# Unused tiles shift where three stages' matmul operands start in SBUF

## The chip, the cores and the metric

The kernel runs on one core of a Trainium2 chip. The metric is the device time of one execution in microseconds (us). The kernel before took 562.35 us, the median of three runs (561.91 to 562.72).

## The reference, cut to what matters

Three layers follow each other, in float32:

```python
# 1. attention, 2 x 8 heads, 768 positions, 64 dims: only keys in the query's hash bucket count
mask   = q_bucket[:, :, :, None] == k_bucket[:, :, None, :]     # 6 bits, sign of q @ proj, k @ proj
scores = np.where(mask, scale * q @ k.T, -1e9)
attn   = exp(scores - max(scores)); x = (attn / (sum(attn) + 1e-9)) @ v
# 2. a dense layer on 1536 tokens of 512
h    = x @ w_in                         # to 1024
solu = h * softmax(h)
ln   = (solu - mean(solu)) / sqrt(var(solu) + 1e-6) * g_ln
x    = ln @ w_out                       # back to 512
# 3. one of 8 experts for each token
e   = argmax(x @ w_gate)
out = gate * sigmoid(x @ w_output_gate)[e] * (relu(x @ w1[e]) @ w2[e])
```

## The kernel before, in words

The order of the work is written out by hand (`tc.manual_schedule()`): each engine runs its instructions in the order in which the functions issue them, and semaphores join the engines.

**Numbers in two parts.** Most products are made of float32r operands: a value x is kept as a high part (tiles whose names begin with H, or end in h) and a low part (L, or l), and a product is the sum of high x high, high x low and low x high. A TensorE matmul here has a stationary operand, which an LDWEIGHTS brings into the array (128 columns of 4 bytes from each partition), and a moving operand that is streamed past it (256, 384 or 512 columns of 4 bytes). In the profile's rows PE is the streaming, PEld the loading of the next stationary operand, which runs beside it. In the names of L243 the moving operand stands first: `ps<-Hk,Hq` streams Hk past Hq.

**Attention** (`Attention`, up to about 208 us). Eight pairs of heads, one in partitions 0 to 63 and one in 64 to 127, so that matmuls come in pairs that run side by side in the two halves of the array (`both`, L239). For each pair of heads `rowmax` (L247) makes masked scores with k moving and q stationary (every third column of q) for VectorE to take row maxima of; `score` (L269) makes them again with q moving and k stationary, four products each (Hk Hq, Hk Lq, Lk Hq, and Fk Fq for the mask and the maximum). ScalarE takes the exponential, GpSimd adds up denominators, `av` (L288) multiplies by v in plain float32. The tiles of q and k come from the pool `op`: `turn` (L174) makes Hk and Hq, `low` (L183) Lk and Lq, `mask` (L222) Fk and Fq, two buffers each.

**The dense layer** (`Ffn`, about 211 to 372 us). Twelve tiles of 128 tokens. `up` (L636) streams the parts of W_in (`wi`) past the parts of x (`xh`, `xl`, pool `xp`); `turn` (L689) transposes the gated activations into `lh` and `ll` (pool `lp`); `down` (L702) streams the parts of W_out (`wo`) past `lh` and `ll`. Both go through `gemm` (L628), whose matmuls stand at L634. The last token tile goes through `down2` with 256 columns at a time.

**The experts** (`Experts`, from about 373 us). Each expert's weights come by DMA, are cut into `wh` and `wl`, and are used twice: `up` (L1216, matmuls at L1231) streams the tokens' `xh` and `xl` (pool `xe`; for expert 0 the two buffers of tile `e` in pool `ep`), 256 columns, past `wh` and `wl`; `down` (L1243, matmuls at L1253) streams `wh` and `wl`, 512 columns, past the hidden values, which lie in W_out's old tiles `wo`.

**Places.** A pool lays its tiles one behind the other in each partition's memory, each at a multiple of 32 bytes, and the pools stand one on the other; so the size of a tile sets where all later ones start. Nothing in the kernel before asks for a certain start.

Of the kernel before, what the change touches and what calls it, by code (L numbers as in the profile page):

```python
# [8 lines left out]
F32 = mybir.dt.float32  # L9
# [7 lines left out]
P = 128  # L17
# [102 lines left out]
class Attention:  # L120
    def __init__(self, tc, ctx, q, k, v, xT):
        self.tc, self.nc = tc, tc.nc
        self.src = dict(q=q, k=k, v=v)
        self.xT = xT
        pool = lambda n, b, **kw: ctx.enter_context(tc.tile_pool(name=n, bufs=b, **kw))
        self.nat = pool("nat", 1)
        self.op = pool("op", 2)
        self.ap = pool("ap", 1)
        self.sp = pool("sp", 2)
        self.st = {}  # L130
        self.pt = []
        pp = pool("pt", 1)
        for i in range(NPT):
            self.pt.append(pp.tile([P, 2, HW + 2], F32, name=f"pt{i}"))
        self.npt = self.nmax = 0
        self.maxima = [pp.tile([P, 3, 2, 3], F32, name=f"m{i}") for i in range(2)]

    def preset(self):
# [5 lines left out]
    def open(self, ctx):  # L144
        self.order = self.pools = [
            ctx.enter_context(self.tc.tile_pool(name=f"ps{n}", bufs=1, space=PSUM)) for n in range(4)
        ]
        self.order = self.pools[1:]
        self.aside = self.pools[0]
        self.filler = self.new(self.aside)[:, 0]  # L150
# [23 lines left out]
    def turn(self, j):  # L174
        nc, st = self.nc, self.st[j]
        for nm in "kq":
            hi = self.op.tile([P, 2, HW], F32R, tag="H" + nm, name="H" + nm)
            nc.scalar.copy(hi, st["T" + nm])
            st["H" + nm] = hi.rearrange("p i n -> p (i n)")
            if j == 0:  # L180
                self.low(0, nm, nc.gpsimd)

    def low(self, j, nm, eng):  # L183
        st = self.st[j]
        t = self.op.tile([P, 2, HW], F32R, tag="L" + nm, name="L" + nm)
        st["L" + nm] = t.rearrange("p i n -> p (i n)")
        eng.tensor_tensor(
            out=st["L" + nm], in0=st["T" + nm].rearrange("p i n -> p (i n)"), in1=st["H" + nm].bitcast(F32), op=ALU.subtract
        )
# [32 lines left out]
    def mask(self, j):  # L222
        nc, st = self.nc, self.st[j]
        ps = [self.wide() for _ in range(2)][::-1]
        for i in range(2):
            for x, o in ((1, D), (0, 0)):
                r = slice(o, o + D)
                nc.tensor.matmul(
                    ps[x][:, i], self.C["tab"][r, i + 2 * x, :], st["bits"][r], start=True, stop=True, tile_position=(o, 0)
                )  # L230
        for x, nm in ((1, "k"), (0, "q")):
            t = self.op.tile([P, 2, HW], F32R, tag="F" + nm, name="F" + nm)
            if x:
                nc.scalar.activation(out=t, in_=ps[x], func=AF.Relu)
            else:
                nc.vector.tensor_copy(t, ps[x])
            st["F" + nm] = t.rearrange("p i n -> p (i n)")

    def both(self, ps, jobs):  # L239
        for n, (w, x) in enumerate(jobs):  # L240
            for h in range(2):
                r = slice(D * h, D * h + D)
                self.nc.tensor.matmul(  # L243
                    ps[:, h], w[r], x[r], start=(n == 0), stop=(n == len(jobs) - 1), tile_position=(D * h, 0)
                )
# [321 lines left out]
def apart(tc, group, ins, gap):  # L567
    ins = ins.ins
    tc.nc.gpsimd.memset(gap, 0.0)
    tc.declare_no_dep(ins, group=group, reason="the rows that these DMAs write are disjoint")  # L570
    tc.add_to_no_dep_group(group, ins)
# [18 lines left out]
class Ffn:  # L590
# [3 lines left out]
    def __init__(self, tc, ctx, C, xT, W, scratch, cnt, ep, ex):  # L594
        self.tc, self.nc, self.C, self.xT, self.ex = tc, tc.nc, C, xT, ex
        self.scratch, self.base, self.W = scratch, cnt, W
        nc = self.nc
        pool = lambda n, b, **kw: ctx.enter_context(tc.tile_pool(name=n, bufs=b, reuse_waits="tile", **kw))
        self.xp = pool("xp", 2)
        self.ep = ep  # L600
        self.lp = pool("lp", 2)
        self.gp = pool("gt", 1)
        self.sp = pool("sp2", 3)
        self.ph = pool("ph", 2, space=PSUM)
        self.pt = pool("ptr", 2, space=PSUM)
        self.py = pool("py", 1, space=PSUM)
        self.pl = pool("pl", 1, space=PSUM)
        self.lg = self.pl.tile([P, 512], F32, name="lg")
        self.st, self.grp, self.sent, self.turned = {}, {}, [], []
        self.wi = W.wi  # L610
        self.wo = W.wo
        self.iota = self.gp.tile([P, CAP], F32, name="iota")
        self.spot, self.st_row, self.split_row, self.low = {}, {}, {}, []
# [475 lines left out]
class Experts:  # L1089
# [23 lines left out]
    def open(self, ctx):  # L1113
        pool = lambda n, b, **kw: ctx.enter_context(self.tc.tile_pool(name=n, bufs=b, reuse_waits="tile", **kw))
        self.rp = pool("rp", 3)
        self.xp = pool("xe", 2)
        self.sp = pool("se", 4)
        self.px = pool("pxe", 2, space=PSUM)
        self.pg = pool("pg", 2, space=PSUM)
        self.po = pool("po", 1, space=PSUM)  # L1120
# [244 lines left out]
@with_exitstack  # L1365
def tile_kernel(
    ctx: ExitStack, tc, q, k, v, proj, moe_w_in, moe_w_out, moe_g_ln, moe2_w_gate, moe2_w_output_gate, moe2_w1, moe2_w2, out
):
    nc = tc.nc
    cp = ctx.enter_context(tc.tile_pool(name="cp", bufs=1))  # L1370
    scratch = tc.dram_tile([SLOTS + N, ROW], F32, name="scratch")
    cnt = cp.tile([P, E], F32, name="cnt")

    def clear(z, n):
        nc.sync.dma_start(
            out=scratch[4 * P * n:4 * P * (n + 1), :].rearrange("(p a) r -> p (a r)", p=P).rearrange("p (b x) -> p b x", b=10),
            in_=z.unsqueeze(1).to_broadcast([P, 10, 2 * ROW // 5]),
        )

    def blank(z):  # L1380
        nc.gpsimd.memset(z, 0.0)
        for n in range(3):
            nc.sync.dma_start(
                out=out[4 * P * n:4 * P * (n + 1), :].rearrange("(p a) r -> p a r", p=P),
                in_=z.unsqueeze(1).to_broadcast([P, 4, DM]),
            )

    with tc.manual_schedule(), ExitStack() as c0, ExitStack() as c4:
        c1 = c0.enter_context(ExitStack())
        xp = c1.enter_context(tc.tile_pool(name="xT", bufs=1, side="right"))  # L1390
        xT = xp.tile([P, 2, 4, S], F32, name="xT")
        keep = c4.enter_context(tc.tile_pool(name="wo", bufs=1))
        W = Weights(tc, cp, xp, keep, moe_w_in, moe_w_out, moe_g_ln, moe2_w_gate, moe2_w_output_gate)
        with ExitStack() as c2:
            cv = c2.enter_context(tc.tile_pool(name="cv", bufs=1))
            at = Attention(tc, c2, q, k, v, xT)
            at.load(0, "qk")
            at.C = C = {}
            at.open(c2)
            make_consts(tc, cp, cv, proj, C)  # L1400
            at.preset()
            nc.gpsimd.tensor_copy(cnt, C["first"])
            nc.gpsimd.memset(W.wg, 0.0)
            at.warm(10)
            at.tables()
            at.warm(1)
            z = cv.tile([P, 2 * ROW // 5], F32, name="zero")
            nc.gpsimd.memset(z, 0.0)
            extra = W.steps(cv, at.bank)
            at.run(8, extra, [lambda n=n: clear(z, n) for n in range(7)])  # L1410
        stg = c4.enter_context(tc.tile_pool(name="ws", bufs=4, reuse_waits="tile"))
        ep = c4.enter_context(tc.tile_pool(name="ep", bufs=2, reuse_waits="tile"))
        r0 = c4.enter_context(tc.tile_pool(name="r0", bufs=1, reuse_waits="tile"))
        ex = Experts(tc, C, stg, moe2_w1, moe2_w2, scratch, out, r0, W.wo)
        with ExitStack() as c2:
            ffn = Ffn(tc, c2, C, xT, W, scratch, cnt, ep, ex)
            for u in range(4):
                ex.fetch(u)

            def ahead():  # L1420
                c1.close()
                return ex.ahead(c0)

            ffn.run(ahead, blank)
        with ExitStack() as c2:
            ex.open(c2)
            ex.run(lambda: counts(tc, C, cnt))
    overflow(tc, C, moe2_w1, moe2_w2, scratch, out, ex.done)
# [36 lines left out]
```

## Time and profile before

| | us |
|---|---|
| median of three runs | 562.35 |
| profiled execution | 562.85 |
| its span, first to last instruction | 561.0 |
| PE busy in the span | 548.5 (98%) |
| DVE, POOL, ACT busy | 394.9, 330.7, 268.4 |

The profiled execution was 0.5 us over the median; 1.85 us of it lie outside its span. A row of a source line gives each kind of instruction with its count and the shortest, median and longest duration of one. A matmul's duration includes a tail that lies under the next matmul, so the time from one start to the next is shorter than the duration. The timeline joins neighbours of the same kind: its second column runs from the first one's start to the last one's end.

### The profile page before, as it was taken

Reading aid. Unit: us, or ns where it says so; the run is one execution under the profiler, and the core shown is the slowest. Engines: PE = TensorE matmul, PEld = TensorE weight load, DVE = VectorE, ACT = ScalarE, POOL = GpSimd, SP = SyncE. Lnnn points to the kernel's source line nnn. Section 1 sums busy time; section 2 is a strip of 40 time slices with the busy share of each in tenths; the row PEclk is TensorE's granted clock in tenths of the full one; section 3 lists DMA queues with packets and bytes.
Section 4 is the critical chain, followed back from the end, with each engine's and each line's share of the span. In section 5 each row is a group of like instructions: output and inputs, shape, how many; then the busy total and the mean of one; then the engine's idle time right before and its main releaser. Section 6 shows DMA issues by size and latency. Waiting matters only on the chain. (4 is left out here: it accounts for less than half of the span.)

```text
span 561.0 us, 9939 instructions
## 1 busy us (share of the span) xinstructions
PE 548.5 (98%) x3850; PEld 437.8 (78%) x3850; DVE 394.9 (70%) x793; ACT 268.4 (48%) x456; POOL 330.7 (59%) x270
## 2 busy tenths in 40 slices
PE   8899999999999999999999999999999999999995
PEld 3776667776667747788888888899989989899894
DVE  7978888888988756766687777776674664656631
ACT  3457657575665651233223323637455463463530
POOL 5389898898989883000000050327785965958741
PEclk9899999999999999999999999999999999999999
DMA  3555636465452535600000040139829467497201
GB/s 112 155 148 146 161 128 194 135 160 145 158 143 81 129 108 221 224 1 1 1 1 0 1 96 0 76 101 365 301 74 339 141 243 258 152 332 253 78 23 36
DMA packets 48100, 76.09 MB, mean 136 GB/s; under 512 B 11563, under 2 KB 20523, under 8 KB 48046
## 3 DMA queue, kind: packets, MB, share of 16 engines
q1 hardware_dynamic: 42910, 59.50, 33.3%
q10 hardware_dynamic: 2896, 9.57, 5.6%
q0 software_dynamic: 2240, 6.31, 3.5%
q8 instruction: 32, 0.52, 0.4%
q14 instruction: 22, 0.18, 0.1%
HBM read 58.39 MB, written 17.93 MB: 136 GB/s over the span
## 5 line engine op out<-in xcount | busy, mean ns | idle before, releaser
L1143 POOL TENSOR_TENSOR wl<-ws,wh 128x512 fp32r<-128x512 f32 x75 | 107.5, 1467 | 40.1 <-ACT wh L1141 39.4
L283 POOL TENSOR_TENSOR acc<-pt,pt 128x768 f32<-128x768 f32 x48 | 89.9, 1873 | 29.3 <-ACT pt L279 29.3
L255 DVE TENSOR_REDUCE m<-ps 128x2 f32<-128x768 f32 x96 | 87.9, 949 | 12.0 <-PE ps L243 9.5
L279 ACT ACTIVATE pt<-ps 128x768 f32<-128x768 f32 x96 | 76.4, 813 | 38.1 <-PE ps L243 38.0
L1253 PE MATMUL o<-wh,wo 128*128 128x512 f32 x256 | 82.5, 394 | 0.0
L1141 ACT CAST wh<-ws 128x512 fp32r<-128x512 f32 x120 | 66.2, 619 | 6.0 <-POOL wl L1143 4.7
L294 PE MATMUL ps<-pt,v 128*64 128x385 f32 x384 | 67.1, 493 | 0.0
L616 POOL TENSOR_TENSOR xl<-xT,xh 128x512 fp32r<-128x512 f32 x12 | 15.4, 1288 | 86.4 <-ACT xh L625 56.3
L1143 DVE TENSOR_TENSOR wl<-ws,wh 128x512 fp32r<-128x512 f32 x45 | 53.8, 1222 | 10.5 <-ACT wh L1141 10.3
L1237 DVE SCALAR_TENSOR_TENSOR wo<-g,wo 128x512 fp32r<-128x512 f32 x32 | 22.1, 691 | 51.9 <-ACT wo L1236 51.9
L285 POOL TENSOR_TENSOR acc<-acc 128x768 f32<-128x768 f32 x30 | 54.8, 1827 | 2.4
L1253 PEld LDWEIGHTS o<-wh,wo 128*128 128x128 f32 x256 | 48.1, 188 | 9.7
L1236 ACT ACTIVATE wo<-g 128x512 fp32r<-128x512 f32 x32 | 19.1, 598 | 75.1 <-PE g L1231 69.4
L294 PEld LDWEIGHTS ps<-pt,v 128*64 128x64 f32 x384 | 25.6, 136 | 34.3 <-issue 30.4
L1253 PE MATMUL o<-wl,wo 128*128 128x512 f32 x128 | 50.1, 391 | 0.0
L634 PE MATMUL h<-wi,xh 128*128 128x512 f32 x192 | 49.4, 399 | 0.0
L634 PE MATMUL y<-wo,lh 128*128 128x512 f32 (+1 forms) x176 | 41.5, 387 | 0.0
L634 PEld LDWEIGHTS h<-wi,xh 128*128 128x128 f32 x192 | 34.9, 188 | 7.4 <-ACT xh L625 0.6
L797 POOL DMA_INDIRECT scratch<-row,slot x12 | 12.0, 999 | 48.3 <-DVE slot L824 23.2
L243 PE MATMUL ps<-Hk,Hq 64*128 64x384 f32 x192 | 37.0, 374 | 1.1 <-DVE m L255 0.5
L634 PEld LDWEIGHTS y<-wo,lh 128*128 128x128 f32 x176 | 31.5, 188 | 7.2 <-issue 0.2
L243 PE MATMUL ps<-Hq,Hk 64*128 64x384 f32 x192 | 35.4, 364 | 1.0 <-DVE m L255 1.0
(240 smaller groups left out, 1157.4 us busy)
## 6 DMA issues: line engine op xcount, KB each, us to landing
ws<-in_moe_w_dram SPq DMA_DIRECT2D x32, 1024.0 KB
scratch<-zero SPq DMA_DIRECT2D x7, 1030.0 KB
r<-scratch SPq DMA_DIRECT2D x16, 257.5 KB
raw<-in_moe_w_in_dram ACTq DMA_DIRECT2D x8, 512.0 KB
raw<-in_moe_w_out_dram ACTq DMA_DIRECT2D x8, 512.0 KB
v<-in_v_dram SPq DMA_DIRECT2D x8, 384.0 KB
out_dram<-zero SPq DMA_DIRECT2D x3, 1024.0 KB
q<-in_q_dram SPq DMA_DIRECT2D x7, 384.0 KB
```

What stands on the lines that cost most here:

```text
L243: self.nc.tensor.matmul(ps[:, h], w[r], x[r], start=(n == 0), stop=(n == len(jobs) - 1), tile_position=(D * h, 0))
L255: nc.vector.tensor_reduce(out=st["m", i][:, c, :, kh], in_=ps, axis=AX.X, op=ALU.max, negate=True)
L279: nc.scalar.activation(out=pt[:, :, 0:HW], in_=ps, func=AF.Exp, scale=0.125)
L283: nc.gpsimd.tensor_tensor(out=acc, in0=st["pt", i, c - 1][:, :, 0:HW], in1=pt[:, :, 0:HW], op=ALU.add)
L285: nc.gpsimd.tensor_tensor(out=acc, in0=parts.pop(), in1=acc, op=ALU.add)
L294: nc.tensor.matmul(st["x", i][D * h:D * h + D, 0:HW + 1], st["v"][:, h, c, :], st["pt", i, c][:, h, 0:HW + 1], start=(c == 0), stop=(c == ...
L634: nc.tensor.matmul(ps, a[:, k, :], w[j](k), start=(n == 0), stop=(n == len(jobs) - 1))
L1141: nc.scalar.copy(hi[:, k, :], t[:, k, :])
L1143: eng.tensor_tensor(out=lo[:, k, :], in0=t[:, k, :], in1=hi[:, k, :].bitcast(F32), op=ALU.subtract)
L1236: nc.scalar.activation(out=hi, in_=ps, func=AF.Relu)
L1237: nc.vector.scalar_tensor_tensor(out=hl[:, 2 * g:2 * g + 2, :], in0=ps, scalar=0.0, in1=hi.bitcast(F32), op0=ALU.max, op1=ALU.subtract)
L1253: nc.tensor.matmul(st["o"][t], h[:, f, t * P:(t + 1) * P], w[:, f % 4, :], start=(f == 0 and n == 0), stop=(f == 7 and n == 2),)
```

## The change

Ten tiles that nothing writes or reads are put into pools, and so later tiles start elsewhere:

```diff
+        self.gaps = []                                             # Attention.__init__
...
@@ Attention.turn, behind the low part of the first k and of the first q, and Attention.mask, behind Fk and Fq
             if j == 0:
                 self.low(0, nm, nc.gpsimd)
+                self.apart(16 if nm == "k" else 48)
+
+    def apart(self, n):
+        self.op.tile([P, n], F32, tag=f"apart{n}{len(self.gaps)}", name="apart", bufs=1)
+        self.gaps.append(n)
...
             st["F" + nm] = t.rearrange("p i n -> p (i n)")
+            if j == 0:
+                self.apart(16 if nm == "k" else 48)
...
@@ Ffn.__init__
         self.lp = pool("lp", 2)
         self.gp = pool("gt", 1)
+        self.lp.tile([P, 56], F32, name="shift", bufs=1)
+        self.gp.tile([P, 8], F32, name="rest")
...
@@ Experts.open
         self.xp = pool("xe", 2)
+        self.xp.tile([P, 8], F32, name="shift", bufs=1)
...
@@ tile_kernel
         r0 = c4.enter_context(tc.tile_pool(name="r0", bufs=1, reuse_waits="tile"))
+        ep.tile([P, 8], F32, name="shift", bufs=1)
+        r0.tile([P, 56], F32, name="rest")
```

The starts of the matmuls' operands in a partition, modulo 256 bytes, as the built programs have them:

| stage | moving | stationary | before: moving, stationary | after |
|---|---|---|---|---|
| scores, `score` | Hq, Lq, Fq | Hk, Lk, Fk | 128, 128 | 192, 128 |
| scores, `rowmax` | Hk, Fk | Hq, Fq | 128, 128 | 128, 192 |
| W_in product | wi | xh, xl | 224, 224 | 224, 224 |
| W_out product | wo | lh, ll | 160, 224 | 160, 192 |
| experts' `up` | xh, xl, e | wh, wl | 160, 224 | 192, 224 |
| experts' `down` | wh, wl | hidden, in wo | 224, 160 | 224, 160 |

The slices that one matmul reads begin whole multiples of 256 bytes further on (in `rowmax` the stationary ones 0, 4 or 8 bytes beyond that). Tiles behind the new ones that are not in the table move by 256 or 512 bytes, or by 32 bytes more or less; some, like `lt` and `id`, are small.

The instructions of PE, DVE, ACT and POOL are the same, in the same order and with the same waits. On SP the order of the DMAs is the same too; what differs is which of them waits. In what is executed the one place is in the experts' `rows`, which loads the routed tokens of experts 1 and 2 (`r`, four DMAs) into memory that earlier tiles leave. Before:

```order
L1185 DMA r_4515<-scratch 128x515 [waits DMAHW3_49,DVE_49,PE_49]
L1185 DMA r_4518<-scratch 128x515 [waits DMAHW4_49,DVE_49,PE_49]
L1185 DMA r_4521<-scratch 128x515 [waits DMAHW5_49]
L1185 DMA r_4524<-scratch 128x515 [waits DMAHW6_49]
L1130 DMA ws<-in_moe_w_dram 128x4x512 [waits DVE_49] x2
```

And with the change:

```order
L1196 DMA r_4524<-scratch 128x515 [waits DMAHW3_49,DVE_49,PE_49]
L1196 DMA r_4527<-scratch 128x515 [waits DMAHW4_49,PE_49]
L1196 DMA r_4530<-scratch 128x515 [waits DMAHW5_49]
L1196 DMA r_4533<-scratch 128x515 [waits DMAHW6_49,DVE_49,PE_49]
L1141 DMA ws<-in_moe_w_dram 128x4x512 [waits DVE_49] x2
```

The wait for DVE that stood ahead of the second DMA now stands ahead of the fourth, with one for PE.

## Rows read from the trace of the kernel before

**Rows 1.** Busy time of the engines in attention, dense layer, experts.
```profile
core 0: us, PE busy (x) PEld busy (x) DVE busy (x) ACT busy (x) POOL busy (x), PEclk, DMA share, GB/s
13.00:208.00 195.00, 192.04 (x1659) 132.39 (x1659) 160.96 (x219) 120.50 (x177) 166.46 (x92) 0.99 0.51 143
224.00:366.00 142.00, 141.32 (x805) 116.89 (x804) 104.17 (x341) 48.58 (x95) 20.98 (x28) 1.00 0.13 41
374.00:545.00 171.00, 171.00 (x1160) 156.46 (x1161) 102.47 (x139) 86.14 (x160) 123.43 (x105) 1.00 0.61 212
```

**Rows 2.** What PE waited for, longest in total first.
```profile
PE ps L243 <- DVE m L255: 1.5, 3, 1.0
PE ps L228 <- DVE bits L220: 1.4, 2, 0.9
PE ps L195 <- DVE fill L46: 1.3, 1, 1.3
```

**Rows 3.** Timeline of PE, W_in product: start, length, what, count.
```profile
213.87 1.98 PE L634 MATMUL h<-wi,xh 128*128 128x512 f32 x8
...
222.03 1.30 PE L634 MATMUL h<-wi,xh 128*128 128x512 f32 x5
```

**Rows 4.** Timeline of PE, W_out product.
```profile
241.70 3.89 PE L634 MATMUL y<-wo,lh 128*128 128x512 f32 x16
```

**Rows 5.** Timeline of PE, experts' up.
```profile
397.95 0.62 PE L1231 MATMUL g<-xh,wh 128*128 128x256 f32 x4
...
403.85 0.62 PE L1231 MATMUL g<-xh,wl 128*128 128x256 f32 x4
```

**Rows 6.** Timeline of PE, experts' down.
```profile
407.93 0.62 PE L1253 MATMUL o<-wh,wo 128*128 128x512 f32 x2
...
411.36 0.62 PE L1253 MATMUL o<-wh,wo 128*128 128x512 f32 x2
```

**Rows 7.** Timeline of PE, attention's scores.
```profile
149.84 0.34 PE L243 MATMUL ps<-Hk,Hq 64*128 64x384 f32 x2
...
150.55 0.34 PE L243 MATMUL ps<-Hq,Hk 64*128 64x384 f32 x2
...
151.24 0.34 PE L243 MATMUL ps<-Hk,Hq 64*128 64x384 f32 x2
151.42 0.34 PE L243 MATMUL ps<-Fk,Fq 64*128 64x384 f32 x2
```

**Rows 8.** Matmuls by line and form: busy us, mean ns.
```profile
L195 PE MATMUL ps<-fill 64*128 64x512 bf16 x2 | 0.6, 376 | 0.0
```

**Rows 9.** Timeline of PE, two bfloat16 filler matmuls.
```profile
7.91 0.59 PE L195 MATMUL ps<-fill 64*128 64x512 bf16 x2
```

**Rows 10.** Line 634, the dense layer's products: shortest, median, longest ns.
```profile
L634 PE MATMUL h<-wi,xh x192: 387/393/501, 211.0 to 342.8; 128*128 128x512 f32 x192
L634 PE MATMUL y<-wo,lh x176: 276/394/496, 229.3 to 362.2; 128*128 128x512 f32 x160, 128*128 128x256 f32 x16
L634 PE MATMUL y<-wo,ll x88: 281/394/400, 233.0 to 364.0; 128*128 128x512 f32 x80, 128*128 128x256 f32 x8
L634 PE MATMUL h<-wo,lh x32: 276/379/484, 351.7 to 366.3; 128*128 128x512 f32 x16, 128*128 128x256 f32 x16
L634 PE MATMUL h<-wo,ll x16: 276/338/398, 356.3 to 367.2; 128*128 128x512 f32 x8, 128*128 128x256 f32 x8
```

**Rows 11.** Line 1231, experts' up, the same columns.
```profile
L1231 PEld LDWEIGHTS g<-xh,wh x224: 187/188/188, 396.3 to 543.0; 128*128 128x128 f32 x112
L1231 PE MATMUL g<-xh,wh x224: 276/276/280, 396.6 to 543.1; 128*128 128x256 f32 x112
L1231 PE MATMUL g<-e,wh x64: 276/276/388, 373.3 to 384.6; 128*128 128x256 f32 x64
```

**Rows 12.** Line 243, attention's scores; below, what PE and PEld waited for there.
```profile
L243 PE MATMUL ps<-Hq,Lk x192: 330/331/518, 18.5 to 206.1; 64*128 64x384 f32 x192
...
  DVE m L255: 7.4, 15
```

**Rows 13.** Timeline of SP, the experts' first rows.
```profile
377.35 1.78 SPq L1185 DMA_DIRECT2D r<-scratch  x4
```

**Rows 14.** Line 1200, the transposes that read such rows.
```profile
L1200 PE MATMUL x<-ident,r x56: 271/272/273, 391.6 to 529.0; 128*128 128x128 f32 x56
```

## The prediction

> **What bounds the kernel now.** I read the engines' busy time by stage first. In attention PE is busy 192.0 of 195 us, in the dense layer 141.3 of 142, among the experts 171 of 171, at a granted clock of 0.99 to 1.00, its upper level; no other engine is over 85% in any of them [rows 1]. The list of waits agrees: the longest that PE itself waited for one cause is 1.5 us in total [rows 2]. So the end is set by how fast matmuls follow each other, and the next view is the timeline of PE, from which I take the time from one start to the next, and divide it by the columns streamed, to compare stages:
>
> - W_in product: 36 matmuls of 512 columns start between 213.87 and 222.03, so 226.7 ns each, 0.443 ns a column [rows 3].
> - W_out product: 16 take 3.89 us with the last one's 0.394 [rows 4, 10], so (3.89 - 0.394) / 15 = 233.1 ns, 0.455 a column.
> - Experts' up: 52 of 256 columns between 397.95 and 403.85, 113.5 ns, 0.443 a column [rows 5].
> - Experts' down: 15 between 407.93 and 411.36, 228.7 ns, 0.447 a column [rows 6].
> - Attention's scores: 9 pairs of 384 columns between 149.84 and 151.42, 175.6 ns a pair, 0.457 a column; the four pairs of `rowmax` before 150.55 take 177.5 each [rows 7].
> - bfloat16 filler, half as many bytes a column: 0.59 - 0.376 = 0.214 us for 512, 0.418 a column [rows 8, 9].
>
> Products of the same kind of operands thus run at 0.443 to 0.457 ns a column, 3% apart, and the filler 6% below the best. Nothing in the waits explains that: streaming itself is slower in places, while the next stationary operand is read from the same memory beside it. Where the operands start is one thing that differs between these stages. The two stages with the highest figure, attention and W_out, are both touched by the change, and so is experts' up, which has the lowest.
>
> **The change part by part.** It adds and removes no instruction. What it can do is alter these spacings, and a change of one is felt in full, since PE has no slack to absorb it.
>
> Attention: 6 kinds of 192 matmuls, 576 pairs. If q's new place brings them to the lowest level that such operands have, 0.4427 x 384 = 170.0 ns, a pair gains 5.6 ns: 576 x 5.6 = 3.2 us. The shortest typical duration among them, 331 ns for Hq past Lk [rows 12], shows that some already run near that. Bounds: at the filler's 0.418, 160.5 ns, the gain is 15.1 x 576 = 8.7 us; upward, W_out's product, whose operands lie 64 apart as these now will, runs 0.0125 ns a column over W_in's, whose lie at 0, and that on 384 columns is 4.8 ns, a loss of 2.8 us. I take 3.2, the level that two other stages hold steadily. Not all is kept: the weight loads of these lines already wait 7.4 us in 15 places for VectorE's maxima [rows 12], and a faster `rowmax` arrives earlier. I give back half of what its 192 pairs gain, 0.5 us. GpSimd and VectorE, at 166 and 161 of 195 us [rows 1], can follow a stage that is 1.4% shorter.
>
> W_out: 160 + 80 + 16 + 8 = 264 matmuls of 512 columns [rows 10]. From 233.1 to 226.7 ns is 6.4 x 264 = 1.7 us. Bounds: at the filler's 214 ns 5.0 us gained; one more such step upward, 1.7 lost. The 48 of 256 columns are at 276 to 281 ns at their shortest [rows 10], the same as experts' up, and count nothing.
>
> Experts' up: 8 experts x 8 blocks x 12 = 768 matmuls, at 276 ns median with hardly any spread [rows 11]. They are at the lowest level already, so I take 0. Bounds: at the filler's rate 107 ns, 6.5 x 768 = 5.0 us gained; at the 281 ns that is the shortest of `y<-wo,ll` [rows 10], which has the same width, 5 x 768 = 3.8 us lost.
>
> W_in's product and experts' down keep their distance: 0. VectorE, ScalarE and GpSimd also read and write the shifted tiles; no row has such an operand at another start, but they are idle 15% of a stage or more [rows 1], which covers a few per cent. The moved SP waits cost nothing: the four loads are issued within 1.78 us from 377.35, and what reads them first starts at 391.6 [rows 13, 14]; were DVE's wait late there, the weights queued behind on SP would be late too, but SP passed that same wait as its second of four.
>
> Sum: 3.2 - 0.5 + 1.7 = 4.4 us off the profiled execution's 562.85, and since that stood 0.5 us over the median, 562.35 - 4.4 = 558.0 as the median of runs.
>
> **One rule against it.** The Trainium skill, page "SBUF — State Buffer", section "Who interferes with whom", gives TensorE two read ports, one for the moving operand and one for LDWEIGHTS, that are independent, and says that PE never waits on anyone. No run here shows ports; by that rule there would be no conflict between the operands and the gain would be 0. The skill's page "TensorE: Matmul & The Clock Gate", section "Back-to-back issue gap", gives N / 2.4 + 2.5 ns, an estimate of 215.8 for 512 columns: the filler's 214 agrees, the 226.7 and 233.1 of the float32r products do not, so something takes 11 to 17 ns more.
>
> **The rivals.**
>
> *Start addresses do nothing.* For it: distance does not sort the rows. Stationary 64 above moving gives 0.455 in W_out and 0.443 in experts' up; equal starts give 0.443 in W_in and 0.457 in attention. The differences could come from width, from the half-array pairs, or from the strided q. Against it: W_in and W_out have the same shape and width and alternate on the same engine, and only places differ. Time: 562.4. This is also what the first of the skill's two rules would give.
>
> *Distance 64 is the bad one.* W_out is the only 512-wide product with the stationary operand 64 above the moving, and is slower than the one at 0 of the same shape. `rowmax` gets just that distance, `score` the same one downward. Then attention loses its 2.8 us, W_out at 32 recovers half of its 1.7, and the time is 562.35 + 2.8 - 0.8 = 564.4; if experts' up also leaves its level, for 281 ns, it is 568.2. I take 566 for it. It decides once attention's pairs are over 177 ns. Against it: experts' up has this distance too, and is at the lowest level.
>
> *The lowest level is itself a conflict.* Then the moved stages could go below 0.443, towards the filler's 0.418. All three at the filler's rate would give 8.7 + 5.0 + 5.0 = 18.7 us, and half of that 553.0. For it: the filler's rate on the same array. Against it: four stages at three distances end within 1% of 0.445, and a float32r column is twice the bytes.
>
> **How the numbers follow.** Forecast, 1.2 to 8 us gained: 0.43. No effect: 0.22. Distance 64 bad: 0.23. Below the lowest level: 0.12. About 0.2%, 1.1 us, is what a measurement can tell from no change; so faster 0.43 + 0.12 = 0.55, same 0.22, slower 0.23. The likeliest case alone runs from 554.5 to 561. The range goes to 551, past the middle of the last rival, and to 566.5, past that of the slower one, which leaves out about 0.06 and 0.09.
>
> **What would show it.** Right: medians of L243 at about 331 to 333 throughout, and L634's `y<-wo,lh` at 389 instead of 394, with L1231 still at 276 and L1253 and `h<-wi,xl` as now. No effect: the same medians to the nanosecond. The slower rival: L243's medians up by 4 or more, L1231 over 277. Below the level: L1231 under 274 or L634 under 386. The forecast is wrong as a whole if the medians fall and the span does not, for then PE was not the bound; longer waits for VectorE's maxima would show it.

## The result, and the profile after

The changed kernel takes 566.13 us, the median of four runs (565.68 to 566.33); beside them the kernel before took 562.54 (561.91 to 563.16). The ratio is 1.0061, with a 95% interval of 1.0049 to 1.0074: 3.6 us slower, where 4.4 us faster was forecast. The profiled execution took 565.97 us, its span is 564.3.

The same windows by stage as [rows 1] come first (us, then busy us and count for PE, PEld, DVE, ACT, POOL; granted clock, DMA share, GB/s).

```profile
13.00:208.00 195.00, 191.82 (x1662) 131.29 (x1663) 161.89 (x220) 120.67 (x177) 166.99 (x92) 1.00 0.51 143
224.00:366.00 142.00, 141.32 (x805) 117.12 (x805) 104.27 (x340) 49.03 (x96) 20.67 (x26) 1.00 0.13 41
374.00:545.00 171.00, 171.00 (x1134) 156.54 (x1133) 101.50 (x137) 85.16 (x158) 123.06 (x104) 1.00 0.61 212
```

PE is as full as before and its clock stands at the same upper level. But among the experts it gets through 1134 matmuls in 171 us instead of 1160: it is busy throughout, and each step takes longer. Which step is seen in the rows by line (count, shortest/median/longest ns, first and last start, forms), the answers to [rows 10 to 12].

```profile
L1242 PE MATMUL g<-xh,wh x224: 277/280/285, 396.6 to 546.3; 128*128 128x256 f32 x112
...
L1242 PE MATMUL g<-e,wh x64: 277/280/386, 372.8 to 384.6; 128*128 128x256 f32 x64
...
L644 PE MATMUL y<-wo,lh x176: 277/395/500, 228.8 to 361.7; 128*128 128x512 f32 x160, 128*128 128x256 f32 x16
...
L644 PE MATMUL h<-wi,xl x96: 388/389/397, 212.5 to 343.2; 128*128 128x512 f32 x96
...
L251 PE MATMUL ps<-Hq,Lk x192: 328/332/337, 18.7 to 205.6; 64*128 64x384 f32 x192
...
  DVE m L263: 8.7, 21
```

Experts' `up` (L1231 before) went from a median of 276 to 280 ns. W_out's product (L634 before) did not go from 394 to 389 but to 395. The untouched W_in product stays at 389; the row of before, from the same view as [rows 10]:

```profile
L634 PE MATMUL h<-wi,xl x96: 388/389/398, 213.0 to 343.7; 128*128 128x512 f32 x96
```

In attention Hq past Lk stays within 1 ns, and the wait for VectorE's maxima rose from 7.4 us in 15 places to 8.7 in 21.

The timeline of PE gives the spacing from start to start, as in [rows 4, 5].

```profile
241.23 3.90 PE L644 MATMUL y<-wo,lh 128*128 128x512 f32 x16
...
397.99 0.63 PE L1242 MATMUL g<-xh,wh 128*128 128x256 f32 x4
...
403.67 0.63 PE L1242 MATMUL g<-xh,wh 128*128 128x256 f32 x4
```

W_out: (3.90 - 0.395) / 15 = 233.7 ns, the same level as before. Experts' `up`: 48 steps in 5.68 us are 118.3 ns, against 113.5 before. There are 768 such matmuls: 768 x 4.8 = 3.7 us. That is the whole loss, and the starts of the stages put it in the same place:

| from the trace, us | before | after |
|---|---|---|
| first W_in matmul | 211.0 | 210.5 |
| first matmul of experts' `up` | 373.3 | 372.8 |
| last start of `g<-xh,wh`, experts' `up` | 543.1 | 546.3 |
| dense layer | 162.3 | 162.3 |
| experts | 169.8 | 173.5 |

### The profile page after: what moved, and what is told of

It reads as the page before. It is cut to its first block, busy times and chain, and to the rows that moved or that the text cites. A ratio compares the mean times of both kernels' runs of the same rounds, so it can differ in the third digit from the quotient of the medians.

```text
span 564.3 us, 9940 instructions
## 1 busy us (share of the span) xinstructions
PE 552.0 (98%) x3850; PEld 440.2 (78%) x3850; DVE 394.9 (70%) x793; ACT 268.6 (48%) x456; POOL 330.9 (59%) x270
```

## The experiments

In what follows the *distance* is the start of the stationary operand minus that of the moving one, modulo 256 bytes. Before, it is 0 in W_in's product, 64 in W_out's, 64 in experts' `up`, 192 in `down`; the change makes it 32 in W_out's and in `up`. My theory after the result was that the spacing depends on the distance. The rivals were that the moving operand's own start decides, that odd and even multiples of 32 differ, and that the places do nothing and the experts are slower for another reason. Spacings below are taken from all starts of a stage in the trace; where a fence shows only durations, a matmul's duration is its spacing plus the tail of some 163 ns (276 for 113.5, 281 for 118).

**Experts' places put back, and these places alone.** The first kernel is the changed one without three of its tiles, the second the kernel before with only those three.

```diff
 # Experts.open
-        self.xp.tile([P, 8], F32, name="shift", bufs=1)
 # tile_kernel
-        ep.tile([P, 8], F32, name="shift", bufs=1)
-        r0.tile([P, 56], F32, name="rest")
```

> The changed kernel without the experts' two shifts: attention's q stays 64 bytes beside k and lh, ll stay 32 beside W_out, but the experts' x goes back to its old start, 64 below the weights. If the loss is the experts' up alone (768 matmuls at about 118 instead of 113.4 ns, 3.5 us), the time is 562.5 less what attention gained (its scores took about 1 us less from first to last in the changed kernel): 561.5, and matmuls of experts' up last 276 ns again. If the loss is spread or lies in the waits, most of it stays: 564 to 566.

> The kernel before with the experts' two shifts alone (x 32 below the weights instead of 64). If the experts' up is the loss: 562.5 + 3.5 = 566.0 or somewhat more (attention's gain is missing), with 280 ns matmuls in experts' up. If the loss needs the other shifts too: 562.5.

Without the three tiles: 562.34 us against 562.45, ratio 0.9997 (0.9988 to 1.0006). With them alone: 565.89, ratio 1.0054 (1.004 to 1.0069). The rows of the experts' `up` line, first the one, then the other:

```profile
L1241 PE MATMUL g<-xh,wh x224: 276/276/281, 396.4 to 542.9; 128*128 128x256 f32 x112
```

```profile
L1232 PE MATMUL g<-xh,wh x224: 277/280/285, 396.5 to 546.2; 128*128 128x256 f32 x112
```

So the loss is the experts' part, whole. The first time is not the 561.5 that was expected, so it also says that the other two parts together are worth nothing measurable: -0.1 us, at most 0.7 gained and 0.3 lost. With the attention of before, the second kernel starts its dense layer at 210.50, the changed one at 210.53; the half microsecond between those and the 211.01 of before is thus no gain of attention's new places. From the first to the last matmul of the scores the kernel before took 198.5 us in its trace, but 197.7 in the second kernel here, with the same places; with q moved, in the changed kernel, 197.5.

**The distance swept in two ways.** The first kernel gives the experts' x, W_out's stationary `lh`, `ll` and attention's q another start in each expert, token tile and pair of heads. The second sweeps the experts' x and W_in's x, with the experts' weights 32 bytes lower, so that the same start of x gives another distance, and the same distance comes from other starts.

```diff
 # Experts.turn, both (and likewise Ffn, Attention)
-        xh = st["xh"] = self.xp.tile([P, 4, CAP], F32R, tag="xh", name="xh")
+        o = ([0, 0, 8, 16, 24, 32, 48, 56])[e]
+        wide = [self.xp.tile([P, 4 * CAP + 64], F32R, tag=n, name=n) for n in ("xh", "xl")]
+        xh, xl = (t[:, o:o + 4 * CAP].rearrange("p (k n) -> p k n", k=4) for t in wide)
 # Experts.ahead, the second only
+        self.wp.tile([P, 8], F32, name="shift", bufs=1)
```

> One look at many starts at once; each pair of heads, token tile and expert has another start, so the time itself says little. Experts 1 to 7 read x that starts at 160, 192, 224, 0, 32, 96, 128 modulo 256, with the weights at 224: distances 64, 32, 0, 224, 192, 128, 96. Theory distance: odd multiples of 32 (32, 224, 96) give about 118 ns, the even ones (64, 0, 192, 128) 113.4. Theory line: what counts is the moving operand alone, good at 32 beyond a multiple of 64; here it gives the same pattern, and the next run separates the two. Theory one good place: only distance 64 gives 113.4 and all others 116 to 120. W_out: lh and ll start at 224, 0, 32, ... for token tiles 0, 1, 2, ...; theory distance expects a change at even multiples against odd ones, theory line expects 233 ns throughout, since W_out's own start does not move. Attention: q at 128, 160, ... for pairs of heads 0, 1, ...: theory distance expects pairs of heads 1, 3, 5, 7 slower than 0, 2, 4, 6.

> The same starts of the experts' x, with the weights' tiles 32 bytes lower (192): distances for experts 1 to 7 are 32, 0, 224, 192, 160, 96, 64. Theory distance: now experts 2, 4, 7 (0, 192, 64) are at 113.4 ns and 1, 3, 5, 6 at 118. Theory line: as in the other sweep, experts 1, 3, 5, 6 (x at 160, 224, 32, 96) at 113.4 and 2, 4, 7 at 118. Experts' down streams the moved weights past the old W_out tiles, distance 224 instead of 192: theory distance expects more than 229 ns, theory line too (the moving operand now starts at a multiple of 64). W_in: xh and xl start at 224, 0, 32, ... for token tiles 0, 1, 2, ..., with wi in its place: theory distance expects token tiles 1, 3, 5, ... over 227 ns, theory line 227 throughout.

First kernel, matmuls by form (busy us, mean ns), one window for each of experts 1 to 4, at distances 64, 32, 0, 224; then its timeline of PE, W_out's low part in token tiles 0, 2, 4 and 6, at distances 64, 128, 192, 0:

```profile
L1241 PE MATMUL g<-xh,wl 128*128 128x256 f32 x32 | 4.9, 276 | 0.0
L1241 PE MATMUL g<-xh,wl 128*128 128x256 f32 x32 | 5.1, 281 | 0.0
L1241 PE MATMUL g<-xh,wl 128*128 128x256 f32 x32 | 5.1, 283 | 0.0
L1241 PE MATMUL g<-xh,wl 128*128 128x256 f32 x32 | 5.1, 279 | 0.0
```

```profile
232.75 2.03 PE L641 MATMUL y<-wo,ll 128*128 128x512 f32 x8
...
257.61 2.02 PE L641 MATMUL y<-wo,ll 128*128 128x512 f32 x8
...
283.64 2.00 PE L641 MATMUL y<-wo,ll 128*128 128x512 f32 x8
...
309.41 1.98 PE L641 MATMUL y<-wo,ll 128*128 128x512 f32 x8
```

Second kernel, the same views: experts 1 to 3, at distances 32, 0, 224, so with the x of the first kernel's first three; and W_in's low part at distances 0 and 64.

```profile
L1237 PE MATMUL g<-xh,wl 128*128 128x256 f32 x32 | 5.1, 281 | 0.0
L1237 PE MATMUL g<-xh,wl 128*128 128x256 f32 x32 | 5.1, 283 | 0.0
L1237 PE MATMUL g<-xh,wl 128*128 128x256 f32 x32 | 5.0, 279 | 0.0
```

```profile
212.56 1.07 PE L637 MATMUL h<-wi,xl 128*128 128x512 f32 x4
...
218.06 1.10 PE L637 MATMUL h<-wi,xl 128*128 128x512 f32 x4
```

With all distances of both (ns from start to start):

| distance | 0 | 32 | 64 | 96 | 128 | 160 | 192 | 224 |
|---|---|---|---|---|---|---|---|---|
| 256 columns, first | 119.9 | 118.3 | 113.4 | 118.7 | 120.0 | | 117.8 | 116.7 |
| 256 columns, second | 119.9 | 118.3 | 117.8 | 118.7 | | 119.9 | 117.8 | 116.8 |
| 512 columns, W_out, first | 228.5 | 232.8 | 233.4 | 234.1 | 232.5 | 233.7 | 229.5 | 233.1 |
| 512 columns, W_in, second | 228.9 | 232.7 | 233.4 | 233.2 | 232.1 | 232.9 | 229.8 | 233.1 |

The sequence 281, 283, 279 moved by one expert with the weights: it goes with the distance. The moving operand's own start does not decide, nor do odd and even multiples. Two products with other operands agree within 1 ns at each distance. A third product agrees: `down` is at 229.1 ns at 192, in the kernel before, and at 233.2 at 224, in the second sweep. Experts' `up` had stood at 64, the only distance at which this table has 113.4. W_out went from 64 to 32, two bad ones for 512 columns; its good one is 0. One entry did not fit: 64 gave 113.4 in one kernel and 117.8 in the other. An entry is one or two experts or token tiles of a single trace, so another level at the other distances is not ruled out. In attention the pairs of `score` were between 173.7 and 176.3 ns by pair of heads in the first sweep, those of `rowmax` between 175.1 and 178.2; the kernel before, at one distance throughout, has 174.5 to 176.0 and 175.9 to 179.7.

**Distance 0 for the 512-column products.** If the table holds, moving W_out's tiles to 224 puts both its product and the experts' `down` (whose hidden values lie there) at 0.

```diff
 # the changed kernel, without its tiles in Ffn, Experts and tile_kernel; Weights.__init__, ahead of and behind wo
+        keep.tile([P, 16], F32, name="shift")
+        keep.tile([P, 48], F32, name="rest")
```

> Both sweeps give the same spacing at the same distance (stationary start minus moving start, modulo 256) in W_in and W_out: 0 is best for 512 columns (226.7 to 229 ns), then 192 (229.5), all others 232 to 234; for 256 columns 64 is the only one under 116. So: W_out's tiles 64 bytes higher, at 224, where lh, ll and the experts' weights start too, which makes the distance 0 in W_out's product and in the experts' down; attention's q stays 64 beside k, the experts' x as in the kernel before. Theory distance: W_out 264 matmuls from 233.3 to 227, 1.7 us; experts' down 384 from 229.2 to 227, 0.9 us; attention by its spacings 384 x 1.1 + 192 x 1.6 ns = 0.7 us, of which the run with the experts put back kept little: 559.2 to 559.9. If the other operands' places or waits had made the sweeps' differences, it stays at 562.4.

Measured: 563.06 us, ratio 1.0007 (0.9998 to 1.0016). Both products did go down, W_out from 233.3 to 227.5 ns and `down` from 229.1 to 227.1. But experts' `up`, in which nothing had moved, went up, by form and by line:

```profile
L1263 PE MATMUL o<-wl,wo 128*128 128x512 f32 x128 | 49.9, 390 | 0.0
...
L644 PE MATMUL y<-wo,lh 128*128 128x512 f32 x160 | 38.5, 393 | 0.0
```

```profile
L1241 PE MATMUL g<-xh,wh x224: 280/282/282, 394.0 to 542.8; 128*128 128x256 f32 x112
...
L1241 PE MATMUL g<-e,wh x64: 275/277/386, 370.8 to 382.1; 128*128 128x256 f32 x64
```

Expert 0 has 277, the seven others 282 (117.8 ns), at an unchanged distance of 64: 672 x 4.3 = 2.9 us lost, against 264 x 5.8 = 1.5 and 384 x 2.0 = 0.8 us gained; the sum, 0.6 us over the 562.61 of the kernel before, is what was measured to 0.2 us. The distance alone is therefore not the whole of it. The second level is the one that the second sweep had shown at 64.

**Finer steps, and 64 at other places.** One kernel sweeps in steps of 4 to 16 bytes; the other holds the distance at 64 in experts 1 to 7, but with x and weights both at other starts.

```diff
 # finer steps: Experts.turn, Ffn.turn
+        o = ([0, 1, 63, 62, 60, 4, 2, 6])[e]
...
+        o = ([48, 49, 50, 52, 54, 47, 46, 44, 42, 34, 30, 48])[i]
...
 # 64 elsewhere: Experts.turn, with the weights 32 bytes lower
+        o = ([56, 56, 56, 56, 56, 56, 56, 56])[e]
```

> One look at distances that are no multiples of 32. Experts 1 to 7 have 60, 68, 72, 80, 48, 56, 40 instead of 64. W_out: 0, 4, 8, 16, 24, 252, 248, 240, 232, 200, 184, 0 for token tiles 0 to 11. Attention: q 64, 68, 72, 80, 60, 56, 48, 64 beside k for the eight pairs of heads. If two streams of 64-byte pieces meet (spacings settle at multiples of 16 columns: 544 and 560 cycles for 512, 272 for 256), a shift of 4 to 16 bytes changes the spacing little, since each stream waits for the next piece; then 60 to 72 stay at 113.4 and the others come near their neighbours' 118. If single 4-byte columns meet, every step of 4 bytes gives another value, and some may be under 113.3 and 226.7.

> The kernel before with the experts' weights 32 bytes lower (192) and the x of experts 1 to 7 32 lower too (128), so that their distance of 64 is kept at another place; expert 0's x stays, at distance 32. In the last sweep one expert with just these places stood at 117.8 ns instead of 113.4. If distance alone decides, that was one of two rhythms that distance 64 can fall into, and at least some of the seven experts fall into the 113.4 of the kernel before. If the place counts too (both operands now start at a multiple of 64), all seven are at 117.8. Expert 0 at 118.3 either way. Experts' down is at distance 224: 233 ns.

Finer steps by form, experts 1, 2 and 7, at distances 60, 68 and 40:

```profile
L1241 PE MATMUL g<-xh,wl 128*128 128x256 f32 x32 | 5.3, 288 | 0.0
L1241 PE MATMUL g<-xh,wl 128*128 128x256 f32 x32 | 5.1, 280 | 0.0
L1241 PE MATMUL g<-xh,wl 128*128 128x256 f32 x32 | 5.2, 286 | 0.0
```

Four bytes under 64 the spacing is 123.2 ns, the worst of all, four over it 118.4; at 56 it is 120.5, at 72 it is 120.1. With 512 columns 0 settles at 226.7, 4 gives 232.4, 252 gives 233.5, and a second good one stands at 240, with 226.7. The distance counts to within 4 bytes, and not only by multiples of 32. Attention shows it here too: the pairs of `score` are at 172.5 ns with q 60 bytes beside k and at 177.4 with 72.

64 elsewhere by form, experts 1 to 4:

```profile
L1234 PE MATMUL g<-xh,wl 128*128 128x256 f32 x32 | 4.9, 276 | 0.0
L1234 PE MATMUL g<-xh,wl 128*128 128x256 f32 x32 | 5.1, 281 | 0.0
L1234 PE MATMUL g<-xh,wl 128*128 128x256 f32 x32 | 4.9, 276 | 0.0
L1234 PE MATMUL g<-xh,wl 128*128 128x256 f32 x32 | 5.1, 281 | 0.0
```

Experts 1, 3 and 6 run at 276, the four others at 281, with the same starts throughout. So at distance 64 two rhythms last, 113.4 and 117.8 ns, and one expert's 96 matmuls settle in one within the first few and stay in it.

The starts in the traces sort the two. From the last matmul of `down` to the first of the next expert's `up` 233 ns pass ahead of experts 1, 3 and 6 here, and 231 ahead of the other four. In all traces together, of the experts behind a `down` with `up` at distance 64 and nothing put between, the 32 with 233 to 236 ns there are in the fast rhythm (the seven of the kernel before among them), and the 12 with 226 to 232 in the slow one, among them the seven of the kernel with `down` at distance 0. So the rhythm goes with how `down` hands over; no run changes that step alone. At distance 32, on the other hand, all 20 experts in the traces are at 118.3 or 118.4 ns, 15 of them with 235 or 236 at that step: the loss of the changed kernel is one of distance and not of rhythm.

**The disputed steps by themselves.** Blocks of 24 identical float32r matmuls were put behind the warm-up, each behind one filler matmul, with another distance, count of stationary columns m or width n.

```diff
+        for m, n, o in self.BLOCKS:
+            self.warm(1)
+            for _ in range(24):
+                self.nc.tensor.matmul(self.filler[0:m, 0:n], st["Hk"][:, o:o + m], st["Hq"][:, 0:n], start=True, stop=True)
```

> The kernel before with 16 blocks of 24 matmuls put in ahead of attention (about 70 us more; their results are not used). Each streams Hq past a slice of Hk, after one filler matmul; stationary columns, streamed columns, distance: 128,512,0; 128,512,64; 128,512,192; 128,512,32; 64,512,0; 64,512,64; 64,512,192; 32,512,64; 128,256,64; 128,256,0; 64,256,64; 64,256,0; 128,512,256; 128,512,320; 128,256,320; 128,512,1024. Theory reads that meet (the stream loses time to the weight load that reads the same memory beside it): the same spacings as in the kernel at 128 stationary columns (227, 233, 229, 233, and 113.4 or 118, 120 for 256), repeated at 256, 320 and 1024, and less than 0.443 ns a column with 64 or 32 stationary columns, towards 214 ns for 512. Theory stream: 0.443 ns a column is what streaming float32r costs, and only what lies above it depends on distance: 64 and 32 stationary columns give 226 to 227 at any distance. Theory of other places: the bench's spacings have nothing to do with the kernel's at the same distance.

Its timeline of PE: 512 columns at distances 0, 64, 192, 32; with 64 stationary columns at 0 and 64; 256 columns at 64 and 0; 64 stationary columns at 0; and 512 columns at 256 and 320.

```profile
8.79 5.84 PE L208 MATMUL ps<-Hq,Hk 128*128 128x512 f32 x24
...
14.51 5.95 PE L208 MATMUL ps<-Hq,Hk 128*128 128x512 f32 x24
...
20.34 5.85 PE L208 MATMUL ps<-Hq,Hk 128*128 128x512 f32 x24
...
26.07 5.94 PE L208 MATMUL ps<-Hq,Hk 128*128 128x512 f32 x24
...
31.89 5.87 PE L208 MATMUL ps<-Hq,Hk 128*64 128x512 f32 x24
...
37.65 5.93 PE L208 MATMUL ps<-Hq,Hk 128*64 128x512 f32 x24
...
54.95 3.17 PE L208 MATMUL ps<-Hq,Hk 128*128 128x256 f32 x24
...
58.01 3.21 PE L208 MATMUL ps<-Hq,Hk 128*128 128x256 f32 x24
...
64.18 3.09 PE L208 MATMUL ps<-Hq,Hk 128*64 128x256 f32 x24
...
67.15 5.84 PE L208 MATMUL ps<-Hq,Hk 128*128 128x512 f32 x24
...
72.87 5.95 PE L208 MATMUL ps<-Hq,Hk 128*128 128x512 f32 x24
```

Settled, these are 226.7 ns at 0, 233.3 at 64, 228.9 at 192 and 233.3 at 32, which are the kernel's own levels; 256 repeats 0 and 320 repeats 64. So it takes neither the dense layer nor the experts to bring the pattern about, and it has a period of 256 bytes. 256 columns at 64 ran in the slower rhythm here, 117.8. Loading 64 stationary columns instead of 128 changed which distance ran fast (256 columns at 0: 113.3 instead of 120.0), but nothing came below 0.443 ns a column, with 64 or with 32. No theory on record held whole: with 64 or 32 stationary columns 512 columns took 228.3 to 232.5 ns, neither less than 226.7, as the theory of reads that meet has it, nor 226 to 227 at any distance, as the theory of the stream has it. The rival of the prediction by which the lowest level is itself a conflict finds no support in that.

**Distance 0 for W_out alone, and another start of `up`.** The first kernel moves `lh` and `ll` onto W_out's start, keeps attention's q where the changed kernel has it, and leaves the experts as before. The second is the kernel with distance 0 in both 512-column products, with a short matmul of 32, 64, ... columns ahead of each expert's `up` from expert 1 on, which is overwritten; it should only shift the moment at which the 96 begin.

```diff
 # Ffn.__init__ (without the changed kernel's tiles in Experts and tile_kernel)
+        self.lp.tile([P, 48], F32, name="shift", bufs=1)
+        self.gp.tile([P, 16], F32, name="rest")
...
 # Experts.up, second kernel
+            if g == 0 and e:
+                nc.tensor.matmul(ps[:, 0, 0:32 * e], wh[:, 0, 0:P], xh[:, 0, 0:32 * e], start=True, stop=True)
```

> The kernel before with attention's q 64 bytes beside k as in the changed kernel and lh, ll at W_out's own start (distance 0); the experts' tiles as before, so that experts' down stays at distance 192 and hands over to experts' up as before. Distance and rhythm: W_out 264 x 6.5 ns = 1.7 us gained, the 48 narrow ones 3 ns slower each, 0.1 us, attention 0 to 0.7; experts' up stays in its 113.4 ns rhythm: 560.3 to 561.0. If experts' up falls into its other rhythm (117.8) whatever precedes it, 563 to 564.

> The version with distance 0 in W_out and experts' down, in which experts' up stood at 117.8 ns in experts 1 to 7, with one short matmul ahead of each of their ups (32, 64, ... 224 columns for experts 1, 2, ... 7; its result is overwritten). No place changes. Rhythm theory: at distance 64 there are two lasting rhythms, and the moment at which the stream starts decides; so some of the seven experts are now at 113.4 ns. If the place of W_out's tiles or the distance in experts' down sets the spacing of up, all seven stay at 117.8.

W_out alone: 561.18 us (560.6 to 561.43), ratio 0.9973 (0.9963 to 0.9984), ahead of both kernels and just over the 560.3 to 561.0 that was expected. Its rows by line:

```profile
L644 PE MATMUL y<-wo,lh x176: 278/389/496, 228.2 to 359.9; 128*128 128x512 f32 x160, 128*128 128x256 f32 x16
```

```profile
L1241 PE MATMUL g<-xh,wh x224: 276/276/280, 394.5 to 541.1; 128*128 128x256 f32 x112
```

The median of 389 is the one that the prediction had named, and the spacing fell from 233.3 to 227.7 ns: 264 x 5.6 = 1.5 us, measured 1.3 (0.9 to 2.1). Experts' `up` keeps its good rhythm.

The shifted moment, by form, experts 0 to 3, one window for each; without the short matmuls expert 0 had stood at 277 and the seven others at 281 or 282:

```profile
L1243 PE MATMUL g<-e,wl 128*128 128x256 f32 x30 | 4.8, 281 | 0.0
...
L1243 PE MATMUL g<-xh,wl 128*128 128x256 f32 x32 | 5.1, 281 | 0.0
L1243 PE MATMUL g<-xh,wl 128*128 128x256 f32 x32 | 4.9, 276 | 0.0
L1243 PE MATMUL g<-xh,wl 128*128 128x256 f32 x32 | 4.9, 276 | 0.0
```

Experts 2, 3 and 6 came to the good rhythm, 1, 4, 5 and 7 stayed in the other. That fits a part of the beginning in the choice, but does not show it: expert 0, which has no short matmul ahead of it and the same program up to there, went from 113.4 to 117.8 ns as well. It starts with pauses in both traces (four steps of 221 to 267 ns among its first eleven), so its beginning differs too, but from one execution to the other. There is one trace of each kernel. Its single time, 563.53 us, includes the added matmuls.

## Why the prediction was wrong

*What bounds the kernel* was right where matmuls follow each other without waits: 3.7 us in `up` stand against 3.6 measured, 1.5 in W_out at distance 0 against 1.3. In attention, where weight loads wait for VectorE's maxima, shorter pairs were not felt. One reading was a little off, GpSimd being busy for 85.4% of attention, not under 85.

*Experts' `up`: "They are at the lowest level already, so I take 0."* This is the step that failed first, and the mis-sized term that made the kernel slower: 0 taken, 3.7 us lost. The other 4.4 us of the 8.0 between forecast and result are the two gains below, which did not come. One step stands under all three terms: a new place was taken to bring a stage to the lowest level or to leave it there, although no row showed a stage at distance 32, or attention at any but 0. Being at the lowest level was read as having nothing to gain; it also meant that any move away could only lose. The row for the bound was there (281 ns at the same width, 3.8 us lost [rows 10]), and it came within 0.1 us by luck, since that row is of another product, at the distance 64 that `up` was about to leave. The sum gave no weight to that leaving; only the slower rival had it, as an *if*.

*W_out: 1.7 us gained.* It gained none: 32 is as bad as 64 for 512 columns (232.8 against 233.4 in the sweep). The premise under it, that the difference to W_in's product comes from the places, holds: at W_in's own distance 0 W_out went to 227.7 ns and 1.3 us were measured. The 226.7 that it took for W_in is that of a settled stretch; over the whole trace W_in's steps are 229.2 ns in the mean.

*Attention: 3.2 - 0.5.* Next to nothing. The pairs did get shorter, `rowmax` from 177.7 to 176.2 ns and `score` from 175.0 to 173.9, which would be 192 x 1.5 + 384 x 1.1 = 0.7 us, not 3.2: the level of 0.443 ns a column, taken over from full-height products, is not reached here at any distance of the sweeps, where the least was 172.5 ns. That Hq past Lk lasts only 331 ns did not show that it ran near that level: its steps to the next pair are 175.1 ns in the trace of before, a shorter duration and not a shorter step. Of the 0.7 the runs can show none; the wait for VectorE's maxima grew by 1.3 us, which the prediction had named as the return.

*W_in, `down` and the SP waits: 0.* Right: W_in's 389 and `down`'s 229.1 ns stayed, and the stage table leaves no room for a late load.

*The rivals.* That places do nothing is refuted: one stage with the same instructions runs at 113.3 to 123.2 ns by its distance. No effect was also what the prediction drew from the Trainium skill's page "SBUF — State Buffer", section "Who interferes with whom", by which PE's two reads are independent and PE never waits on anyone; the runs disagree with that forecast, by up to 9.9 ns in a matmul of 256 columns, while no run shows the ports themselves. The slower rival had the side, and the price of `up` as an *if* in its sum, but not the mechanism: 64 is a bad distance for 512 columns and the good one for 256. That its 566 is nearly the time measured is luck: it lies between 564.4 and 568.2, both of which count 2.8 us lost in attention that were not lost. Its case against itself, that `up` has this distance and is at the lowest level, was the clue. Against the rival below the lowest level the prediction counted four stages within 1% of 0.445; there were three (W_in, `up`, `down`), and the bench is the better ground.

*Left open.* Whether the two reads meet, and where in the memory or the engine; why 64 is good for 256 columns and 0 and 240 for 512; and what sets the rhythm at the start, beyond the step from `down` that goes with it. That the distance matters, with the period and to the 4 bytes, is shown; a conflict between the two reads as its cause is only argued.

## What to carry to other kernels

When PE streams without waits, compare ns a column between stages of the same kind; a few per cent of difference between products of one shape can be the start of the stationary operand against that of the moving one, modulo 256 bytes. Such an offset is not good or bad by itself: it depends on the width, so each stage has to be measured, and the stage that is already at the lowest level is the one to leave alone. Measure after any move of tiles that the stages that did not move kept their spacing, because a stage can change its rhythm without a change in its own places.

## What the runs showed of the hardware

- Identical float32r matmuls that follow each other without waits differ by their operands' distance: 226.7 to 234.1 ns for 512 columns, 113.3 to 123.2 for 256, with a period of 256 bytes; 4 bytes already change it (226.7 at 0, 232.4 at 4).
- At one distance two rhythms can last, 113.4 and 117.8 ns, through 96 matmuls; experts 1 to 7 were all in the slower one in one kernel and all in the faster one in others, with the same places. The rhythm goes with the step from the matmul ahead: 233 to 236 ns in 32 experts in the faster one, 226 to 232 in 12 in the slower.
- The lowest spacing seen is 0.443 ns a column at both widths with 128 stationary columns, and for 256 columns also with 64. The Trainium skill's page "TensorE: Matmul & The Clock Gate", section "Back-to-back issue gap", gives N / 2.4 + 2.5 ns for the gap of a single matmul, an estimate of 215.8 and 109.2 ns; the best float32r figures here are 226.7 and 113.3.
- Half-height pairs of 384 columns in `score` took 172.5 to 177.4 ns by distance, and 174.5 to 176.0 from one pair of heads to the other at one distance.
